# Attention followed by two feed-forward layers on one core: earlier narrowing of the first weights, a first product begun ahead of the last pair's values, and one set of subtractions moved and reordered

## The chip, the cores and the metric

The kernel runs on one core of one Trainium2 chip. The metric is device time in microseconds (us) of one execution. Before the change three runs took 783.86, 786.02 and 790.22 us, with a median of 786.02 us.

A core has five engines that run side by side, each through its own list of instructions in the order in which the program wrote them: PE (TensorE, matrix products; its weight loads are shown as PEld), DVE (VectorE), ACT (ScalarE), POOL (GpSimd) and SP (SyncE, which here issues nearly all DMAs). They wait for one another by semaphores.

## What is computed

The reference is attention with a learned bias on the position, then a feed-forward layer with a rational activation, then four ReLU experts that are mixed by given probabilities. Cut to what matters (B=2, 8 heads, S=576, head width 64; 1152 tokens of 512):

```python
scores = scale * q @ k^T + bias(pos)          # 16 pairs of (batch, head)
attn = exp(scores - max); attn /= sum(attn) + 1e-9
x = (attn @ v) as [1152, 512]
h = x @ w_in                                  # 512 -> 2048, w_in and w_out are float64
P = a0 + a1*h + a2*h^2 + a3*h^3
Q = 1 + |b0|*|h| + |b1|*h^2
x = (P / (Q + 1e-6)) @ w_out                  # 2048 -> 512
out = sum over e of p[:, e] * (relu(x @ w1[e]) @ w2[e])   # 4 experts, 512 -> 1024 -> 512
```

Products are made to float32 accuracy from operands that are split into a high part and a low part (the rest), so that each product is three passes: high by high, high by low, low by high.

## The kernel before, in words

**Attention.** The work is cut into eight pairs of heads, `pair[0]` to `pair[7]`, each of nine units `u` (score blocks of 128 rows by 576). A loop over all units in one row keeps three of them in flight: `scores` two units ahead (PE, two halves of a block into two PSUM buffers called `s`, then on DVE L527, which adds the bias and finds the minimum), `exp` one unit ahead (ACT, L536), then `weights` (DVE, a transpose, L543) and `fill` for the unit itself. `fill` puts other work into the gaps: the products with V of the pair before (`values`, PE, L576), the transposes of q and k of the pair after next (`prep`, only in pairs 0 to 5; the slot in pairs 6 and 7 is empty), the DMAs of later pairs, and POOL's `put`, which divides by the row sums and splits the result into high and low parts of `x` (L594 to L598). Work that `fill` puts on the list `later` is issued at the next unit, ahead of that unit's `exp` and transpose.

**Narrowing.** `w_in` and `w_out` arrive as 64-bit words (tile `words`) and are turned into float32 (tile `narrow`) in four steps: step 0 on ACT (L359), steps 1, 2 and 3 on DVE (L361, L363, L365); step 4 is the split (high part on ACT, L369; low part on POOL, L375). The first two weights are narrowed in four pieces during attention by `early_convert`. The list `EARLY` names the 20 units after which one step each is put on `later`. All four pieces use the one buffer `narrow0`. The loads of the two weights are issued at units (2, 4) and (3, 4), the loads of the next two at (5, 6) and (7, 3). The first piece's result goes to the buffer that held part of the bias of pairs 0 to 3.

**From attention to the first layer.** After the loop the last pair's products with V are made in two calls of `values` (blocks 0 to 4, then 5 to 17), with the first product of the feed-forward layer, `first(W1[0][0], 0)`, between them: 24 matrix products, from four slices `x_t[0]` to `x_t[3]` of the input (slice 3 comes from pairs 6 and 7), into one PSUM buffer `hp`. `chain` then makes the activation from `hp` on ACT and DVE.

**The last expert products.** Two thirds of the tokens go through the experts by a scheme of seven products in place of eight (class `Square`), on sums and differences of the blocks of `x` and of the weights. `sums_of_x` makes these sums, and splits them: high parts on ACT (L953), low parts on DVE (L956, six subtractions). It is a generator that is taken three steps further at three places. `turns(n)` makes n steps of the preparation of the next weight (for a `Group`: ACT L406 and L407, DVE L410, POOL L412 to L415, ACT L417, DVE L420). A `Square`'s first product goes to a PSUM bank `sa`, which ACT copies out (L1046) before PE writes it again.

Of the kernel before, what the change touches and what calls it, by code (L numbers as in the profile page):

```python
# [11 lines left out]
F32 = mybir.dt.float32  # L12
# [9 lines left out]
E, FE = 4, 1024  # L22
# [3 lines left out]
P = 128  # L26
# [5 lines left out]
CHN = 384  # L32
# [15 lines left out]
def attention_then_two_ffn(ctx: ExitStack, tc: tile.TileContext, q, k, v, w1, b1, w2, w_in, w_out, ca, cb, probs, e_w1, e_w2, c_l, c_l8, c_p, c_x, out):  # L48
# [6 lines left out]
    def mm(o, l, r, start, stop):  # L55
        pe.matmul(o, lhsT=l, rhs=r, start=start, stop=stop)  # L56
# [17 lines left out]
    def blk(slot, shape, dt, name):  # L74
        return long.tile(shape, dt, tag=f"blk{slot}", name=name)
# [97 lines left out]
    def catch_up(calls):  # L173
        now, calls[:] = calls[:], []
        for f in now:
            f()
# [517 lines left out]
    COPY_V.update({(n, 1): n for n in range(2, NN)})  # L694
    EARLY_LOAD = (2, 4), (3, 4)
    MORE_LOAD = (5, 6), (7, 3)
    EARLY = [divmod(t + d, 9) for t in (36, 44, 52, 60) for d in (0, 1, 2, 3, 5)]

    units = [(n, u) for n in range(NN) for u in range(9)]
    units[:11] = [(0, u) for u in (0, 1, 2, 3, 4, 5, 8)] + [(1, 0), (1, 1), (0, 6), (0, 7)]  # L700
# [19 lines left out]
            convert(5 - state["step"])  # L720
        return w.t

    def first(w, c):

        wt = ready(w)
        w.left -= 1
        hp = ps.tile([P, 2, 512], F32, tag="s", name="hp")
        for fi in range(2):
            i = 0
            for cc in range(4):  # L730
                for wpart, xpart in ((0, 0), (0, 1), (1, 0)):
                    mm(hp[:, fi, :CHN], wt[:, cc, wpart, 128 * fi:128 * fi + 128], x_t[cc][:, c, xpart], i == 0, i == 11)
                    i += 1
        return hp[:, :, :CHN]


    NGRP = len(GROUPS)
# [43 lines left out]
    last = pair[-1]  # L781
    while later:
        catch_up(later)
    last.values(range(0, 5))
    begun = chain(0, first(W1[0][0], 0), lambda name: blk(8, [P, 2, CHN], F32, name) if name == "u" else sp_.tile([P, 2, CHN], F32, tag="pq", name=name, bufs=3))
    next(begun)
    last.turn()
    last.values(range(5, NKB))
# [147 lines left out]
    def sums_of_x():  # L936


        def y(d, c):
            return yacc[:, d:d + 2, CHN * c:CHN * c + CHN]  # L940

        y11, y21, y12, y22 = y(0, T1), y(0, T2), y(2, T1), y(2, T2)
        dve.tensor_tensor(y22, y21, y22, ALU.add)
        pool.tensor_tensor(y21, y11, y21, ALU.subtract)
        dve.tensor_tensor(y11, y22, y11, ALU.subtract)
        dve.tensor_tensor(y12, y12, y11, ALU.subtract)
        yield
        sa, sb = (blk(slot, [P, 3, 2, CHN], F32R, "s") for slot in S_SLOT)
        x4 = [x_t[c][:, T2] for c in range(2)]
        split = [(y22, sa[:, 0:2]), (y11[:, 0:1], sa[:, 2:3]), (y11[:, 1:2], sb[:, 0:1]), (y21, sb[:, 1:3])] + [(y12[:, c:c + 1], x4[c].unsqueeze(1)) for c in range(2)]  # L950
        sums.extend([sa[:, 0], sa[:, 1], sa[:, 2], sb[:, 0], sb[:, 1], sb[:, 2]] + x4)
        for s, x in split:
            act.activation(x[:, :, 0], s, AF.Copy)  # L953
        yield
        for i, (s, x) in enumerate(split):
            dve.tensor_tensor(x[:, :, 1], s, f32(x[:, :, 0]), ALU.subtract)  # L956
        yield

# [5 lines left out]
    for u in range(E):  # L964
        for f2 in range(1, 4):
            if (u, f2) != (0, 1):
                expert_first(u, f2)
            turns(PACE.get(u, PACE[1])[f2 - 1])
            if 0 < u < E - 1 and results:
                results.pop(0)()  # L970
        if u + 1 < E:
            expert_first(u + 1, 0)
        for t in range(3):
            expert_second(u, t)
            if (u, t) == (E - 2, 0):
                assert not results
                making = sums_of_x()
            if (u, t) in ((E - 2, 0), (E - 1, 0), (E - 1, 1)):
                next(making)
            turns(PACE.get(u, PACE[1])[3 + t])  # L980

    ffn.close()
    psum.close()
# [159 lines left out]
```

## Time and profile before

| what | before |
|---|---|
| runs | 783.86, 786.02, 790.22 us; median 786.02 us |
| profiled execution, own time | 785.17 us |
| its span, first to last instruction | 783.4 us (1.8 us lie outside) |
| PE busy | 758.9 us, 97% of the span |
| PEld busy | 657.0 us, 84% |
| DVE busy | 550.2 us, 70% |
| ACT busy | 429.2 us, 55% |
| POOL busy | 268.0 us, 34% |
| granted TensorE clock | 0.999 of full speed (the upper level, 2.4 GHz) |
| attention with its bias | 0 to about 184 us |
| feed-forward layer | about 184 to 393 us |
| experts, first third of the tokens, then the rest | about 393 to 529 us, 529 to 783 us |

Busy time is time in which an engine works on an instruction. For PE it includes short waits inside a run of matrix products, since their ends are modelled. An engine's idle time matters only where the engine is what the others wait for; here that is mostly PE.

### The profile page before, as it was taken

How to read it: one execution, taken by the hardware profiler on the slowest of the kernel's cores; microseconds unless marked ns; L12 is line 12 of the kernel's file. 1: busy time of each engine (PE TensorE's matmuls, PEld its weight loads, DVE VectorE, ACT ScalarE, POOL GpSimd, SP SyncE). 2: the span in 40 equal slices, each digit the busy share in tenths (PEclk: the TensorE clock that was granted, in tenths of full speed). 3: DMA queues.
4: the chain of work that ended last, by engine and by line, in shares of the span. 5: the costliest groups of instructions: out<-in, count | busy, mean ns of one | idle time of the engine just before them, and what ended most of it. 6: DMA issues, size and time to landing. Idle time of an engine off the chain costs nothing. (4 is left out here: it accounts for less than half of the span.)

```text
span 783.4 us, 15914 instructions
## 1 busy us (share of the span) xinstructions
PE 758.9 (97%) x6470; PEld 657.0 (84%) x6470; DVE 550.2 (70%) x873; ACT 429.2 (55%) x689; POOL 268.0 (34%) x278
## 2 busy tenths in 40 slices
PE   7998999989999999999999999998999999999998
PEld 4445766657899999999998989988989989988987
DVE  7998878996999999999854544566545544644731
ACT  6986657765899789787823425244413423413510
POOL 0000223452354556643210101217435634723710
PEclk9999999999999999999999999999999999999999
DMA  8899587542142142402223435332212212212201
GB/s 149 193 217 213 119 191 171 133 100 65 54 124 93 57 131 83 160 3 61 74 64 126 144 101 159 108 109 95 81 48 79 85 31 82 82 42 75 73 28 54
DMA packets 83945, 79.41 MB, mean 101 GB/s; under 512 B 38016, under 2 KB 62976, under 8 KB 83200
## 3 DMA queue, kind: packets, MB, share of 16 engines
q1 hardware_dynamic: 83440, 78.39, 37.0%
q8 instruction: 51, 0.84, 0.4%
q14 instruction: 22, 0.18, 0.1%
q10 hardware_dynamic: 432, 0.01, 0.0%
HBM read 59.20 MB, written 2.36 MB: 79 GB/s over the span
## 5 line engine op out<-in xcount | busy, mean ns | idle before, releaser
L56 PE MATMUL hp<-x,wi 128*128 128x384 f32 x888 | 159.7, 337 | 1.5 <-DVE u L777 1.1
L56 PEld LDWEIGHTS hp<-x,wi 128*128 128x128 f32 x888 | 154.0, 188 | 4.1 <-PE yp L56 1.5
L56 PE MATMUL op<-w,h 128*128 128x512 f32 (+1 forms) x600 | 133.1, 382 | 0.6 <-DVE acc L895 0.6
L56 PEld LDWEIGHTS op<-w,h 128*128 128x128 f32 x600 | 109.4, 188 | 22.4 <-DVE acc L895 0.8
L56 PE MATMUL yp<-g_hi,w 128*128 128x384 f32 x384 | 102.1, 336 | 0.3 <-ACT y L832 0.3
L895 DVE SCALAR_TENSOR_TENSOR acc<-op,pr_sb,acc 128x512 f32<-128x512 f32 (+1 forms) x28 | 20.4, 730 | 72.4 <-PE op L56 72.4
L56 PEld LDWEIGHTS yp<-g_hi,w 128*128 128x128 f32 x384 | 69.7, 188 | 1.3 <-ACT yacc L824 0.7
L536 ACT ACTIVATE pq<-pq,nm 128x576 f32<-128x576 f32 x72 | 55.4, 771 | 22.2 <-DVE nm L527 21.9
L56 PE MATMUL yp<-g_lo,w 128*128 128x384 f32 x192 | 64.2, 334 | 0.0
L56 PE MATMUL sc<-ks,qs 64*128 64x288 f32 (+1 forms) x320 | 56.9, 429 | 6.4 <-DVE nm L527 4.6
L527 DVE CUSTOM_DVE_ANT_0 pq<-sc,ba 128x576 f32<-128x576 f32 x72 | 51.4, 745 | 16.2 <-PE sc L56 16.1
L417 ACT ACTIVATE wi<-stage 128x1024 fp32r<-128x1024 f32 x16 | 17.0, 1061 | 80.8 <-POOL stage L415 80.8
L373 POOL TENSOR_TENSOR w<-stage,w 128x256 fp32r<-128x256 f32 x64 | 48.2, 784 | 34.3 <-ACT w L369 34.3
L56 PE MATMUL op<-w,h_hi 128*128 128x512 f32 x192 | 59.2, 389 | 0.0
L757 POOL TENSOR_TENSOR g_lo<-u,g_hi 128x768 fp32r<-128x768 f32 x24 | 45.1, 1881 | 36.9 <-ACT g_hi L756 34.9
L369 ACT ACTIVATE w<-stage 128x1024 fp32r<-128x1024 f32 x32 | 33.6, 1054 | 37.4 <-DMA stage<-in_moe_w_dram 37.4
L543 DVE STREAM_TRANSPOSE pt<-pq 128x576 f32<-128x576 f32 x72 | 52.3, 754 | 0.0
L576 PE MATMUL o<-pt,val 32*64 32x128 f32 (+1 forms) x2304 | 48.1, 294 | 2.9 <-issue 1.7
L232 PE MATMUL bps<-hid,wb 128*32 128x288 f32 x576 | 46.9, 410 | 3.9 <-DVE hid L221 3.0
L576 PEld LDWEIGHTS o<-pt,val 32*64 32x64 f32 x2304 | 39.0, 130 | 13.0 <-issue 5.2
L56 PEld LDWEIGHTS sc<-ks,qs 64*128 64x128 f32 (+1 forms) x320 | 29.9, 175 | 23.7 <-DVE nm L527 10.1
L1036 ACT ACTIVATE h<-part_sums 128x384 fp32r<-128x384 f32 x48 | 25.1, 523 | 43.0 <-DVE part_sums L1056 34.4
(141 smaller groups left out, 1444.3 us busy)
## 6 DMA issues: line engine op xcount, KB each, us to landing
stage<-in_moe_w_dram SPq DMA_DIRECT2D x48, 512.0 KB, 3.6
ba<-ev SPq DMA_DIRECT2D x32, 288.0 KB, 5.2
words<-in_moe_w_in_dram SPq DMA_DIRECT2D x8, 1024.0 KB, 5.5
words<-in_moe_w_out_dram SPq DMA_DIRECT2D x8, 1024.0 KB, 5.0
stage<-in_moe_w_dram SPq DMA_DIRECT2D x64, 128.0 KB, 2.4
val<-val SPq DMA_DIRECT2D x21, 288.0 KB, 4.0
val<-in_v_dram SPq DMA_DIRECT2D x11, 288.0 KB, 4.5
out_dram<-acc SPq DMA_DIRECT2D x8, 256.0 KB, 2.0
```

What stands on the lines that cost most here:

```text
L56: pe.matmul(o, lhsT=l, rhs=r, start=start, stop=stop)
L232: pe.matmul(sc[32 * par:32 * par + 32, hf, :288], lhsT=wb.rearrange("p r h -> p (r h)"), rhs=tiles[par][:, 288 * hf:288 * hf + 288], start ...
L369: act.activation(t[:, :, 0, :], self.raw, AF.Copy)
L373: pool.tensor_tensor(t[:, x[0], 1, x[1]], self.raw[:, x[0], x[1]], f32(t[:, x[0], 0, x[1]]), ALU.subtract)
L417: act.activation(s[:, :, 0], raw, AF.Copy)
L527: dve.tensor_tensor_reduce(out=self.row(u + e).rearrange("p (a j) -> p a j", a=2), in0=o[:, :, :288], in1=bs.rearrange("p (a j) -> p a j", ...
L536: act.activation(self.row(u), self.row(u), AF.Exp, bias=least.pop((self.n, u)), scale=-1.0, accum_out=self.sm[:, u:u + 1])
L543: dve.transpose(self.pt[:, 5 * e + k], self.row(u))
L576: pe.matmul(self.o[64 * e:64 * e + 64, a, c:c + 32 * m], lhsT=val[self.n % 2][r, NKB * e + b], rhs=self.pt[r, i:i + m, 32 * b:32 * b + 32] ...
L757: pool.tensor_tensor(lo, u, f32(hi), ALU.subtract)
L895: dve.scalar_tensor_tensor(out=a, in0=op, scalar=pr_sb[:, j, e:e + 1], in1=a, op0=ALU.mult, op1=ALU.add)
L1036: act.activation(t[:, 0], v, AF.Relu)
```

## The change

Three places are edited. The first one moves the steps of the early narrowing: the four pieces start at global units 30, 39, 48 and 57 instead of 36, 44, 52 and 60, that is at unit 3 of pairs 3, 4, 5 and 6. The second one splits the first product of the feed-forward layer: the 18 products on slices 0 to 2 are made ahead of `values(range(0, 5))`, and the six on slice 3 stay behind it. The third one puts the last step of `sums_of_x` behind the three `turns` of its place and takes its six subtractions in another order.

```diff
-    EARLY = [divmod(t + d, 9) for t in (36, 44, 52, 60) for d in (0, 1, 2, 3, 5)]
+    EARLY = [divmod(t + d, 9) for t in (30, 39, 48, 57) for d in (0, 1, 2, 3, 5)]
...
-    def first(w, c):
+    def first(w, c, ccs=range(4), hp=None):
         wt = ready(w)
-        w.left -= 1
-        hp = ps.tile([P, 2, 512], F32, tag="s", name="hp")
+        if hp is None:
+            w.left -= 1
+            hp = ps.tile([P, 2, 512], F32, tag="s", name="hp")[:, :, :CHN]
         for fi in range(2):
-            i = 0
-            for cc in range(4):
+            for cc in ccs:
                 for wpart, xpart in ((0, 0), (0, 1), (1, 0)):
-                    mm(hp[:, fi, :CHN], wt[:, cc, wpart, 128 * fi:128 * fi + 128], x_t[cc][:, c, xpart], i == 0, i == 11)
-                    i += 1
-        return hp[:, :, :CHN]
+                    mm(hp[:, fi], wt[:, cc, wpart, 128 * fi:128 * fi + 128], x_t[cc][:, c, xpart], (cc, wpart, xpart) == (0, 0, 0), (cc, wpart) == (3, 1))
+        return hp
...
+    begun_hp = first(W1[0][0], 0, range(3))
     last.values(range(0, 5))
-    begun = chain(0, first(W1[0][0], 0), lambda name: ...
+    begun = chain(0, first(W1[0][0], 0, range(3, 4), begun_hp), lambda name: ...
...
-        for i, (s, x) in enumerate(split):
+        for s, x in split[1:4] + split[:1] + split[4:]:
             dve.tensor_tensor(x[:, :, 1], s, f32(x[:, :, 0]), ALU.subtract)
...
-            if (u, t) in ((E - 2, 0), (E - 1, 0), (E - 1, 1)):
+            if (u, t) in ((E - 2, 0), (E - 1, 0)):
                 next(making)
             turns(PACE.get(u, PACE[1])[3 + t])
+            if (u, t) == (E - 1, 1):
+                next(making)
```

On DVE, at the turn from pair 6 to pair 7, the fourth piece stood before the change as follows (`pq<-sc,ba` is L527 of one block, `pt<-pq` the transpose of one, `narrow` the piece, L548 and L549 the inverse of pair 6's sums).

```order
L361 TENSOR_SCALAR narrow<-narrow 128x512
L543 STREAM_TRANSPOSE pt<-pq 128x576
L527 ISA pq,nm<-sc,ba 128x576
L527 ISA nm 128x1
L527 ISA pq,nm<-sc,ba 128x576
L527 ISA nm 128x1
L548 TENSOR_SCALAR sm<-sm 128x9
L549 RECIPROCAL sm<-sm 128x9
L363 SCALAR_TENSOR_TENSOR narrow<-words,narrow 128x512
L543 STREAM_TRANSPOSE pt<-pq 128x576
L365 SCALAR_TENSOR_TENSOR narrow<-words,narrow 128x512
L543 STREAM_TRANSPOSE pt<-pq 128x576
```

In the changed program the fourth piece stands here, ahead of pair 6's inverse.

```order
L361 TENSOR_SCALAR narrow<-narrow 128x512
L543 STREAM_TRANSPOSE pt<-pq 128x576
L527 ISA pq,nm<-sc,ba 128x576
L527 ISA nm 128x1
L363 SCALAR_TENSOR_TENSOR narrow<-words,narrow 128x512
L543 STREAM_TRANSPOSE pt<-pq 128x576
L527 ISA pq,nm<-sc,ba 128x576
L527 ISA nm 128x1
L527 ISA pq,nm<-sc,ba 128x576
L527 ISA nm 128x1
L365 SCALAR_TENSOR_TENSOR narrow<-words,narrow 128x512
L543 STREAM_TRANSPOSE pt<-pq 128x576 x2
```

The first step stood between the transposes of units 7 and 8 of pair 6 and now stands between those of units 4 and 5; the second and third stood behind the inverse, among the first units of pair 7, and now stand ahead of the transposes of units 6 and 7. The other three pieces stand in the same way in pairs 3, 4 and 5.

On DVE, where the first third of the tokens ends in the experts, the six subtractions L956 stood before the change between two accumulations L895 and ahead of the Group's L410.

```order
L895 SCALAR_TENSOR_TENSOR acc<-op,pr_sb,acc 128x512
L956 TENSOR_TENSOR s<-yacc,s 128x2x384
L956 TENSOR_TENSOR s<-yacc,s 128x384 x2
L956 TENSOR_TENSOR s<-yacc,s 128x2x384
L956 TENSOR_TENSOR x_1345<-yacc,x_1345 128x384
L956 TENSOR_TENSOR x_1872<-yacc,x_1872 128x384
L410 TENSOR_TENSOR wi<-stage,wi 128x256 x3
L895 SCALAR_TENSOR_TENSOR acc<-op,pr_sb,acc 128x512
L420 TENSOR_TENSOR wi<-stage,wi 128x4x256
```

In the changed program the same place reads:

```order
L895 SCALAR_TENSOR_TENSOR acc<-op,pr_sb,acc 128x512
L410 TENSOR_TENSOR wi<-stage,wi 128x256 x3
L956 TENSOR_TENSOR s<-yacc,s 128x384 x2
L956 TENSOR_TENSOR s<-yacc,s 128x2x384 x2
L956 TENSOR_TENSOR x_1345<-yacc,x_1345 128x384
L956 TENSOR_TENSOR x_1877<-yacc,x_1877 128x384
L895 SCALAR_TENSOR_TENSOR acc<-op,pr_sb,acc 128x512
L420 TENSOR_TENSOR wi<-stage,wi 128x4x256
```

The three L410 went ahead of the six L956, and of the six the two short ones on `s` come first, in the order in which the products take them. ACT and POOL hold the same instructions there in the same order as before.

## Rows read from the trace of the kernel before

**Rows 1.** Busy time by stretch: from:to, length, then each engine's busy time (instructions).

```profile
149.30:164.40 15.10, 13.75 (x334) 9.32 (x334) 13.97 (x33) 11.11 (x28) 6.57 (x9) 1.00 0.46 106
164.40:180.40 16.00, 13.24 (x342) 9.25 (x350) 15.33 (x34) 9.95 (x25) 6.95 (x9) 1.00 0.54 135
```

**Rows 2.** Timeline, PE, pairs 6 and 7: start, length, work, [idle before, ended by].

```profile
159.15 1.91 PE L56 MATMUL sc<-ks,qs 64*128 64x288 f32 x8 [0.73 <-DVE nm L527]
165.12 1.24 PE L56 MATMUL sc<-ks,qs 64*128 64x288 f32 x8 [0.74 <-DVE nm L527]
169.62 1.62 PE L576 MATMUL o<-pt,val 32*64 32x160 f32 x80 [0.50 <-issue]
175.53 1.91 PE L56 MATMUL sc<-ks,qs 64*128 64x288 f32 x8 [1.54 <-DVE nm L527]
```

**Rows 3.** Busy time by stretch of what touches `narrow`: DVE, ACT, POOL.

```profile
149.30:164.40 15.10, 2.07 (x3) 1.32 (x2) 1.28 (x1) 1.00 0.46 106
164.40:180.40 16.00, 2.79 (x3) 1.30 (x2) 1.26 (x1) 1.00 0.54 135
```

**Rows 4.** Timeline, DVE, three narrowing steps.

```profile
144.79 0.64 DVE L365 SCALAR_TENSOR_TENSOR narrow<-words,narrow 128x512 uint32<-128x512 uint32 x1
...
168.45 0.38 DVE L361 TENSOR_SCALAR narrow<-narrow 128x512 uint32<-128x512 uint32 x1
...
172.75 1.37 DVE L365 SCALAR_TENSOR_TENSOR narrow<-words,narrow 128x512 uint32<-128x512 uint32 x1
```

**Rows 5.** Timeline, POOL, when the last of these steps began.

```profile
172.57 1.00 POOL L598 TENSOR_TENSOR x<-x,x 128x384 fp32r<-128x384 f32 x1
```

**Rows 6.** Timeline, DVE, unit 8 of pair 3.

```profile
117.56 0.76 DVE L527 CUSTOM_DVE_ANT_0 pq<-sc,ba 128x576 f32<-128x576 f32 x1 [0.94 <-PE sc L56]
```

**Rows 7.** Timeline, SP, the first weight's load.

```profile
99.80 0.58 SPq L340 DMA_DIRECT2D words<-in_moe_w_in_dram  x1
```

**Rows 8.** One tile's instructions (`words`), 95 to 180 us: its loads.

```profile
DMA to landing us min/median/max: 5.5/6.8/8.3
```

**Rows 9.** Timeline, ACT, an `exp` of pair 3's unit 5.

```profile
112.48 0.76 ACT L536 ACTIVATE pq<-pq,nm 128x576 f32<-128x576 f32 x1
```

**Rows 10.** Timeline, PE, from attention to the first layer.

```profile
180.27 1.64 PE L576 MATMUL o<-pt,val 32*64 32x160 f32 x80
183.03 1.64 PE L576 MATMUL o<-pt,val 32*64 32x160 f32 x80 [1.12 <-ACT x L589]
184.60 4.46 PE L56 MATMUL hp<-x,w 128*128 128x384 f32 x24
...
199.88 4.43 PE L56 MATMUL hp<-x,w 128*128 128x384 f32 x24 [0.85 <-DVE u L777]
```

**Rows 11.** Timeline, POOL, low part of slice 3 of `x`.

```profile
185.18 1.06 POOL L598 TENSOR_TENSOR x<-x,x 128x384 fp32r<-128x384 f32 x1
```

**Rows 12.** Timeline, DVE, around the six subtractions.

```profile
517.83 1.66 DVE L410 TENSOR_TENSOR wi<-stage,wi 128x256 fp32r<-128x256 f32 x3
...
524.65 2.75 DVE L956 TENSOR_TENSOR s<-yacc,s 128x768 fp32r<-128x768 f32 x4
...
528.26 1.09 DVE L410 TENSOR_TENSOR wi<-stage,wi 128x256 fp32r<-128x256 f32 x3
...
533.51 1.23 DVE L420 TENSOR_TENSOR wi<-stage,wi 128x1024 fp32r<-128x1024 f32 x1 [3.49 <-ACT wi L417]
```

**Rows 13.** Timeline, POOL, the Group's four subtractions: first and last.

```profile
528.76 1.19 POOL L412 TENSOR_TENSOR stage<-stage 128x256 f32<-128x256 f32 x1 [7.04 <-DVE wi L410]
...
531.66 0.72 POOL L415 TENSOR_TENSOR stage<-stage 128x256 f32<-128x256 f32 x1
```

**Rows 14.** Timeline, ACT, behind them.

```profile
532.42 1.06 ACT L417 ACTIVATE wi<-stage 128x1024 fp32r<-128x1024 f32 x1 [8.77 <-POOL stage L415]
```

**Rows 15.** Timeline, PE, the same stretch.

```profile
533.90 1.32 PE L1024 MATMUL sa<-x,wi 128*128 128x384 f32 x6 [1.96 <-ACT part_sums L1046]
535.25 1.31 PE L1024 MATMUL sb<-s,wi 128*128 128x384 f32 x6
```

More of the change, by code (lines that the diff above doesn't have):

```diff
@@ L783, in attention_then_two_ffn @@
         catch_up(later)
+    begun_hp = first(W1[0][0], 0, range(3))
     last.values(range(0, 5))
-    begun = chain(0, first(W1[0][0], 0), lambda name: blk(8, [P, 2, CHN], F32, name) if name == "u" else sp_.tile([P, 2, CHN], F32, tag="pq", name=name, bufs=3))
+    begun = chain(0, first(W1[0][0], 0, range(3, 4), begun_hp), lambda name: blk(8, [P, 2, CHN], F32, name) if name == "u" else sp_.tile([P, 2, CHN], F32, tag="pq", name=name, bufs=3))
     next(begun)
```

## The prediction

> **What bounds the kernel now.** I read the share of busy time first: PE works 97% of the span, so a change can gain little more than PE's waits. The list of who waited for whom came next, for PE alone, and PE's timeline to place its waits. Behind the first 80 us most of them lie in three places: in attention's second half, at its end, and at one point in the experts. The chain of waits that ended last is PE alone from 533.9 us to the end, so a shift ahead of that point carries through to the end as long as nothing else becomes late. The granted clock is at the upper level throughout.
>
> Pairs 6 and 7 are the first place. In the two stretches from 149.3 to 180.4 us, 31.1 us long, DVE is busy 29.3 us and PE 27.0 us [rows 1]: DVE is the bound. On PE the reader is to see four waits, 0.73 + 0.74 + 0.50 + 1.54 = 3.51 us [rows 2]. Three end with a `nm` of L527, that is with DVE; I count the one put down to "issue" with them, since these values need pair 6's last transpose, which DVE makes right behind the L361 of 168.45 [rows 4]. In pairs 0 to 5 PE also makes `prep`, so that there DVE waits for PE: 0.94 us ahead of unit 8 of pair 3 [rows 6].
>
> The second place is the end of attention: PE stands idle 1.12 us until ACT has emptied the value bank, then makes values, then the 24 products of `hp` in 4.46 us [rows 10]. The third is a wait of 1.96 us for ACT's L1046 [rows 15]. ACT was held by L417, that by POOL's L412 to L415, those by DVE's L410, and L410 stood behind the six L956 [rows 12, 13, 14].
>
> **First edit, the steps of the narrowing.** No step is added or removed; 12 steps on DVE, 4 on ACT and 4 splits move. In the 31.1 us two pieces stand on DVE, busy 2.07 + 2.79 = 4.86 us [rows 3]. Afterwards only one stands there, the fourth, since the third moves into pair 5. Its price where POOL is idle: 0.38 us for L361, 0.64 us for L365, and the same 0.64 us for L363, which has the same form [rows 4]: 1.66 us. The old price held waits: L365 at 172.75 took 1.37 us, and until 173.57 POOL's L598 was at work [rows 4, 5]. The new places, units 4 to 6, lie ahead of POOL's `put`, which starts after unit 7. So DVE loses 4.86 - 1.66 = 3.20 us, less about 0.07 us by which each of the three steps that leave overlapped its successor: 3.0 us. DVE would then need 26.3 us and PE 27.0 us, which includes short waits; neither is far ahead of the other. I take the gain as DVE's relief, **3.0 us**. From below it is 1.5 us, if only the wait at 175.53 goes; from above 3.5 us, if all four waits of rows 2 go.
>
> What the moved steps cost in pairs 3, 4 and 5: the first piece is new in pair 3, and each piece stands at units 4 to 6. Its second and third step (0.64 us each) precede transposes that nobody on PE needs at once, and DVE's idle time ahead of unit 8 is 0.94 us [rows 6]. I take nothing; without that cover it is 1.66 us a pair. On ACT step 0 (0.65 us, half of ACT's share in rows 3) goes ahead of the `exp` at 112.48 [rows 9]; ACT is idle 4 us of the 15.1 us of a stretch with a piece [rows 1]. It reads the first weight, issued at 99.80 [rows 7], landed at the latest 8.3 us after its issue [rows 8], so by 108.1: 4.4 us early. The single buffer `narrow0` is free again long before the next piece, since POOL's split (1.27 us [rows 3]) follows at the start of the next pair, ahead of nothing but the next `put`, most of a pair later. The load at (7, 3), until now held on SP by the fourth piece's L365, may leave sooner; no other DMA queues behind it before the first layer.
>
> **Second edit, the first product.** The 18 products need no new data: slices 0 to 2 come from pairs 0 to 5, and the PSUM buffer is the one that L527 of unit 8 left. They cost 4.46 / 24 = 0.186 us each, 3.3 us together, and take the place of the wait of 1.12 us; the rest of them is only moved ahead of the values. So the gain is **1.1 us**. It is lost if the six products on slice 3 must wait: they start 3.3 + 1.6 = 4.9 us after the previous values end at 181.9, at 186.8, and the low part of slice 3 was ready at 185.18 + 1.06 = 186.24 [rows 11]. The margin is 0.6 us; the value lies between 0 and 1.1 us. Nothing later takes it back: the activation's chain, `put_last` and the product at 199.88 that waits for L777 [rows 10] all hang on these products and values and move with them.
>
> **Third edit, the subtractions.** PE's wait would go if L412 to L415 ended two us earlier. L410 moves ahead of L956 by the length of the six, 528.26 - 524.65 = 3.6 us [rows 12]. But L412 reads and writes SBUF, and so do L410 and L956, and rows 12 and 13 show that these exclude each other. L412 was started at 528.76, when one L410 was done, and took 1.19 us instead of 0.72: it ended at 529.95, as if it had begun at 529.2, when the third L410 had ended. It waited out two DVE instructions, which follow each other without a gap. After the change the same three L410 are followed without a gap by six L956. If POOL waits out all nine, L412 starts at 524.65 + 1.0 + 3.6 = 529.3, as before, and the edit gives nothing. That is my value: **0 us**. The other bound is the whole wait, 1.96 us, and 0.3 us that the next product (535.25, six products of 0.174 us after 533.90) lost to L1048: 2.3 us.
>
> The Trainium skill, page "SBUF — State Buffer", section "Who interferes with whom", says that a VectorE instruction with two SBUF inputs and a GpSimd instruction that reads SBUF exclude each other, and that whoever issues first holds the pair of ports for one whole instruction. By it L412 would have come in after the second L410; the trace shows it after the third. By the page POOL and DVE would take turns here, which is the first rival below.
>
> **Sum.** The profiled execution took 785.17 us, 1.8 us of it outside the span; 785.17 - 3.0 - 1.1 - 0 = **781.1 us**. It is 0.85 us under the median of the runs shown.
>
> **Rivals.**
>
> *POOL and DVE take turns.* For it: at 517.83 the same three L410 took 1.66 us instead of 1.09 [rows 12], because an L412 came in ahead of the third. Against it: the wait at 528.76. Worked out: L412 to L415 at 0.74 us, an L410 or a short L956 (about 0.4 us) between each two, from 525.1 on, end at about 528.9; L417 ends at 530.0; L1046 is done ahead of 531.8, where PE needs it. DVE then ends L956 at 531.5, makes an L895 (0.7), L420 (1.2 [rows 12]) and L1048 (0.5), so that the product of 535.25 starts at 533.85: 1.4 us gained, **779.7 us**.
>
> *Pairs 6 and 7 find another limit.* PE and DVE feed each other in turns through two PSUM buffers, so that only the wait at 175.53 goes: 785.17 - 1.5 - 1.1 = **782.6 us**.
>
> *Slice 3 comes late.* The second edit gives nothing: 785.17 - 3.0 = **782.2 us**.
>
> *Slower: the narrowing holds up pairs 3 to 5.* Step 2 now stands right behind L527 of unit 8, and step 3 right behind that of the next pair's units 0 and 1; if the transposes behind them are what the next values on PE wait for, each of the three pairs pays the piece's whole 1.66 us, 5.0 us together, and the kernel takes 785.17 - 4.1 + 5.0 = **786.1 us**. It decides from 1.4 us a pair on. For it: DVE is busy most of the time there too. Against it: the idle time in rows 6, just where the steps go.
>
> **How the numbers follow.** I give the forecast 0.45, turns of POOL and DVE 0.25, another limit 0.13, slice 3 late 0.08, the slower case 0.09. The predicted time is 781.1 us. From 778.9 (all of 3.5, 1.1 and a part of the third edit) to 783.7 (1.5 us alone), widened by the 0.85 us between the profiled execution and the median, the range is 778.0 to 784.6 us; it leaves out the slower case and little more. About 1% (7.9 us) is what a measurement of this kernel tells from no change. All upper bounds together, 3.5 + 1.1 + 2.3 = 6.9 us, stay under that, so faster by over 1% gets 0.08, within 1% 0.88 and slower 0.04.
>
> **What would show it.** In the changed profile the stretch between the `rt` products (L561) of pairs 5 and 7 should be about 3 us shorter, and the waits of rows 2 be under 1 us together, with L363 and L365 at about 0.65 us each. Ahead of the values at the end of attention 18 `hp` products should stand without a wait of PE. L412 should start some 3.6 us earlier and still end behind the last L956, with L1046 and PE's wait of 2 us unchanged. The prediction is wrong if the gain of pairs 6 and 7 turns up again as waits in pairs 3 to 5, or if PE's wait for L1046 is gone.

## The result and the profile after

The changed kernel takes 781.05 us (median of 8 runs, 778.51 to 782.72), the kernel before 786.25 us beside it (8 runs). The ratio is 0.992, with a 95% interval of 0.989 to 0.995: 5.2 us less, within 1%. The forecast of 781.1 us lies on the median, but not every term under it was right, and things that I did not forecast took part.

The profiled execution took 778.81 us (span 777.0 us), 6.36 us less than that of before. PE's busy time is what it was, 758.7 us, so all of it is PE's waits. The page's head of the changed kernel (busy us, share of the span, instructions):

```profile
PE 758.7 (98%) x6470; PEld 657.5 (85%) x6470; DVE 551.3 (71%) x873; ACT 428.9 (55%) x689; POOL 266.8 (34%) x278
```

To find where the 6.4 us went I cut both executions at the same PE instructions: the first `rt` product (L561) made in each pair, and the first, seventh and thirteenth product into `sa` of the `Square`s. Ahead of the first cut (100.97 us in both) nothing differs, and behind the last one both need 246.98 us.

| stretch (us) | before | after | difference |
|---|---|---|---|
| `rt` in pair 2 to `rt` in pair 5 | 47.45 | 45.79 | -1.66 |
| `rt` in pair 5 to `rt` in pair 7 | 31.09 | 28.48 | -2.61 |
| `rt` in pair 7 to the last turn's | 9.38 | 8.90 | -0.48 |
| from there to the first `sa` product | 339.75 | 339.61 | -0.14 |
| first to thirteenth `sa` product | 7.75 | 6.25 | -1.50 |

**Pairs 5 to 7.** The two stretches by busy time (from:to, length, then PE, PEld, DVE, ACT, POOL with their instructions, granted clock, share of DMA, GB/s), cut at the `rt` products, of before and then of after; they answer to [rows 1]:

```profile
148.42:163.55 15.13, 13.75 (x336) 9.32 (x334) 14.00 (x32) 10.65 (x28) 6.57 (x9) 1.00 0.52 129
163.55:179.51 15.96, 13.18 (x336) 9.12 (x335) 15.29 (x34) 10.10 (x25) 6.95 (x9) 1.00 0.49 113
```

```profile
146.76:160.26 13.50, 13.11 (x337) 9.12 (x335) 13.15 (x31) 9.54 (x25) 6.03 (x9) 1.00 0.56 140
160.26:175.24 14.98, 13.26 (x336) 9.23 (x335) 14.21 (x33) 10.26 (x26) 6.04 (x9) 1.00 0.45 94
```

DVE is busy 1.93 us less and idle 0.68 us less; together that is the 2.61 us. It is still busy 27.4 of 28.5 us. PE's waits in the changed kernel, from its timeline (start, length, work, [idle before, ended by]), which answer to [rows 2]:

```profile
162.03 1.65 PE L56 MATMUL sc<-ks,qs 64*128 64x288 f32 x8 [0.95 <-DVE nm L527]
...
166.80 1.62 PE L576 MATMUL o<-pt,val 32*64 32x160 f32 x80 [0.38 <-issue]
...
170.70 1.30 PE L576 MATMUL o<-pt,val 32*64 32x160 f32 x50 [0.40 <-issue]
```

Four waits of 3.51 us became three of 1.73 us, and the long one ahead of the last scores is gone. The forecast had wanted them under 1 us together. The twelve steps on DVE, seen as one tile's instructions (`narrow`; ns: shortest, median, longest), answer to [rows 3, 4]:

```profile
L361 DVE TENSOR_SCALAR narrow<-narrow x4: 383/384/386, 114.8 to 160.2; 128x512 uint32<-128x512 uint32 x4
L363 DVE SCALAR_TENSOR_TENSOR narrow<-words,narrow x4: 685/687/689, 117.1 to 161.9; 128x512 uint32<-128x512 uint32 x4
L365 DVE SCALAR_TENSOR_TENSOR narrow<-words,narrow x4: 686/686/686, 120.1 to 164.7; 128x512 uint32<-128x512 uint32 x4
```

No step takes longer than 0.69 us any more, where L365 took 1.37 us beside POOL.

**The end of attention.** PE's timeline, which answers to [rows 10]:

```profile
176.00 2.15 PE L576 MATMUL o<-pt,val 32*64 32x160 f32 x80
178.07 3.39 PE L56 MATMUL hp<-x,w 128*128 128x384 f32 x18
181.40 1.64 PE L576 MATMUL o<-pt,val 32*64 32x160 f32 x80
182.97 1.34 PE L56 MATMUL hp<-x,w 128*128 128x384 f32 x6
```

The 18 products stand where the wait of 1.12 us was, and nothing waits from 176 to 184 us. But the 80 value products at 176.00 take 2.15 us, half a microsecond more than in [rows 10]. The first edit alone will show where that belongs.

**The experts.** DVE, then POOL, then ACT, then PE in the changed kernel, which answer to [rows 12 to 15]. L1046 and L1048 of before are L1048 and L1050 here:

```profile
519.61 1.62 DVE L410 TENSOR_TENSOR wi<-stage,wi 128x256 fp32r<-128x256 f32 x3
521.15 4.39 DVE L956 TENSOR_TENSOR s<-yacc,s 128x384 fp32r<-128x384 f32 x4
525.47 1.01 DVE L956 TENSOR_TENSOR x<-yacc,x 128x384 fp32r<-128x384 f32 x2
526.40 0.74 DVE L895 SCALAR_TENSOR_TENSOR acc<-op,pr_sb,acc 128x512 f32<-128x512 f32 x1
527.07 1.27 DVE L420 TENSOR_TENSOR wi<-stage,wi 128x1024 fp32r<-128x1024 f32 x1
528.26 0.54 DVE L1050 TENSOR_TENSOR part_sums<-sb,part_sums 128x384 f32<-128x384 f32 x1
```

```profile
520.10 0.84 POOL L412 TENSOR_TENSOR stage<-stage 128x256 f32<-128x256 f32 x1 [3.72 <-DVE wi L410]
...
522.92 0.94 POOL L415 TENSOR_TENSOR stage<-stage 128x256 f32<-128x256 f32 x1
```

```profile
525.00 0.49 ACT L1048 ACTIVATE part_sums<-sa 128x384 f32<-128x384 f32 x1
```

```profile
526.88 1.20 PE L1026 MATMUL sa<-x,wi 128*128 128x384 f32 x6
528.86 1.31 PE L1026 MATMUL sb<-s,wi 128*128 128x384 f32 x6 [0.78 <-DVE part_sums L1050]
```

POOL's L412 to L415 are done at 523.86, in the midst of the L956. ACT empties `sa` by 525.5, PE writes it at 526.88 without a wait, and what is late next is `sb`: 0.78 us for L1050, which stands on DVE behind all six L956, L895 and L420. The four L956 on `s` take 4.39 us beside POOL, against 2.75 us alone [rows 12].

### The profile page after: what moved, and what is told of

It is laid out like the page before. It is cut to its first block, busy times and chain, and to the rows that moved or that the text cites. A ratio compares the mean times of both kernels' runs of the same rounds, so it can differ in the third digit from the quotient of the medians.

```text
span 777.0 us, 15918 instructions
## 1 busy us (share of the span) xinstructions
PE 758.7 (98%) x6470; PEld 657.5 (85%) x6470; DVE 551.3 (71%) x873; ACT 428.9 (55%) x689; POOL 266.8 (34%) x278
## 5 line engine op out<-in xcount | busy, mean ns | idle before, releaser
L895 DVE SCALAR_TENSOR_TENSOR acc<-op,pr_sb,acc 128x512 f32<-128x512 f32 (+1 forms) x28 | 20.4, 730 | 72.8 <-PE op L56 72.8
L527 DVE CUSTOM_DVE_ANT_0 pq<-sc,ba 128x576 f32<-128x576 f32 x72 | 51.6, 749 | 13.3 <-PE sc L56 13.1
L417 ACT ACTIVATE wi<-stage 128x1024 fp32r<-128x1024 f32 x16 | 17.0, 1061 | 77.8 <-POOL stage L415 77.8
L576 PE MATMUL o<-pt,val 32*64 32x160 f32 (+1 forms) x2304 | 48.8, 293 | 2.3 <-issue 1.9
L221 DVE TENSOR_SCALAR hid<-tab,cut 128x576 f32<-128x576 f32 x112 | 48.4, 522 | 0.0
```

The costliest lines, as they stand in the source:

```text
L221: dve.tensor_scalar(tiles[par], win, at, 0.0, ALU.add, ALU.max)
L527: dve.tensor_tensor_reduce(out=self.row(u + e).rearrange("p (a j) -> p a j", a=2), in0=o[:, :, :288], in1=bs.rearrange("p (a j) -> p a j", ...
L576: pe.matmul(self.o[64 * e:64 * e + 64, a, c:c + 32 * m], lhsT=val[self.n % 2][r, NKB * e + b], rhs=self.pt[r, i:i + m, 32 * b:32 * b + 32] ...
```

## The experiments

### Each edit alone

The first edit alone:

```diff
-    EARLY = [divmod(t + d, 9) for t in (36, 44, 52, 60) for d in (0, 1, 2, 3, 5)]
+    EARLY = [divmod(t + d, 9) for t in (30, 39, 48, 57) for d in (0, 1, 2, 3, 5)]
```

> The kernel before with the first edit alone (the 20 narrowing steps at the new units). The forecast's own step: pairs 6 and 7 lose 3.0 us, pairs 3 to 5 nothing, so ratio 0.996. Rival: the wait of PE of 1.15 us in pair 3, which the changed kernel's profile no longer has, went because of the moved steps; then 4.3 us and ratio 0.9945. If it was chance, that wait may stand in this trace too. The wait of 1.12 us ahead of the last pair's values and that of 1.96 us for L1046 should both stand as before.

Measured: 783.92 us, ratio 0.9961 (0.9940 to 0.9982). The `rt` products in pairs 5 and 7 are 28.46 us apart, 2.63 us less than before. Pairs 2 to 5 need 47.46 us, as before. But the stretch from pair 7's `rt` to the last turn's grew from 9.38 to 9.91 us, so 2.1 us are left of the 2.63 us. PE's timeline has the slower values of the changed kernel here too, although nothing is split:

```profile
177.64 2.15 PE L576 MATMUL o<-pt,val 32*64 32x160 f32 x80
```

The second edit alone:

```diff
+    begun_hp = first(W1[0][0], 0, range(3))
     last.values(range(0, 5))
-    begun = chain(0, first(W1[0][0], 0), lambda name: ...
+    begun = chain(0, first(W1[0][0], 0, range(3, 4), begun_hp), lambda name: ...
```

> The kernel before with the second edit alone (18 products ahead of the last pair's values). Forecast: the wait of 1.12 us for ACT's L589 goes and nothing takes it back, ratio 0.9986. From the rt products of pair 7 to the last rt products it should take 9.38 - 1.1 = 8.3 us. Rival: the 0.5 us that only came off in the changed kernel's profile (9.38 to 8.90) is all there is, since the values ahead of it lose 0.5 us each time; then 8.9 us here too.

Measured: 786.07 us, ratio 0.9986 (0.9967 to 1.0005). From pair 7's `rt` to the last turn's 8.37 us, 1.01 us less. So it gives its whole price by itself, which the medians alone would not have told.

The third edit alone:

```diff
-        for i, (s, x) in enumerate(split):
+        for s, x in split[1:4] + split[:1] + split[4:]:
...
-            if (u, t) in ((E - 2, 0), (E - 1, 0), (E - 1, 1)):
+            if (u, t) in ((E - 2, 0), (E - 1, 0)):
                 next(making)
             turns(PACE.get(u, PACE[1])[3 + t])
+            if (u, t) == (E - 1, 1):
+                next(making)
```

> The kernel before with the third edit alone (subtractions moved behind the Group's steps and reordered). Forecast: POOL waits out all nine DVE instructions, L412 ends as late as before and PE's wait of 1.96 us stays: 0 us, ratio 1.000. Rival, which the changed kernel's profile speaks for: POOL and DVE take turns, the wait of 1.96 us goes and one of about 0.8 us for the sum on sb (L1048) comes: 1.5 us, ratio 0.998.

Measured: 784.44 us, ratio 0.9964 (0.9943 to 0.9986). First to thirteenth `sa` product 6.26 us, 1.49 us less, with one wait of 0.79 us for L1050. The edit that I had put at nothing gives the second most of the three.

### Which half of the third edit

The move alone, in the old order:

```diff
-            if (u, t) in ((E - 2, 0), (E - 1, 0), (E - 1, 1)):
+            if (u, t) in ((E - 2, 0), (E - 1, 0)):
                 next(making)
             turns(PACE.get(u, PACE[1])[3 + t])
+            if (u, t) == (E - 1, 1):
+                next(making)
```

> The kernel before with one half of the third edit: the step with the six subtractions stands behind the three turns, but the subtractions keep their old order, with the long one (128x2x384, 1.1 us) first and the two short ones that the first products take second and third. Theory one, what counts is that L410 and with it L412 to L415, L417 and L1046 come ahead: PE's wait of 1.96 us for L1046 [rows 15] becomes less than 0.3 us, and from the first to the thirteenth sa product 6.2 to 6.5 us are needed instead of 7.75 (1.3 to 1.5 us gained), as with the whole edit, unless a product waits for its low part. Theory two, the order matters: PE gains a wait for DVE's L956 of 0.5 us or more in the first Square's second half, and the stretch takes 6.7 to 7.3 us. Rival that I took in the prediction (POOL waits out all nine DVE instructions): 7.7 us; the whole edit alone has shown 6.26 us, so that it should not return here.

The new order alone, in the old place:

```diff
-        for i, (s, x) in enumerate(split):
+        for s, x in split[1:4] + split[:1] + split[4:]:
```

> The kernel before with the other half of the third edit: the six subtractions in the new order, but still ahead of the three turns. Theory one, L410 still stands behind six L956 on DVE, so L412 to L415 start as late as before and PE's wait for L1046 stays: 1.96 us, give or take 0.3, and 7.6 to 7.8 us from the first to the thirteenth sa product. Theory two, the gain came from the products finding their low parts earlier: the stretch gets at least 0.5 us shorter. It also shows whether POOL's first L412 waits out two L410 each time at this place (1.19 us in rows 13) or comes in ahead of the third L410, as it did at 517.83 [rows 12].

Measured: the move takes 784.66 us, ratio 0.9978 (0.9960 to 0.9996), the order 786.85 us, ratio 1.0008 (0.9987 to 1.0028). With the move the stretch of the `sa` products is 6.51 us, and PE waits once, 1.03 us for L1050. Its timeline, DVE and PE:

```profile
528.56 1.62 DVE L410 TENSOR_TENSOR wi<-stage,wi 128x256 fp32r<-128x256 f32 x3
...
530.11 4.39 DVE L956 TENSOR_TENSOR s<-yacc,s 128x768 fp32r<-128x768 f32 x4
```

```profile
538.06 1.32 PE L1026 MATMUL sb<-s,wi 128*128 128x384 f32 x6 [1.03 <-DVE part_sums L1050]
```

No product waits for a low part, so theory one holds: the move gives 1.24 of the 1.50 us and the order at most the rest. With the order alone, DVE, POOL and PE:

```profile
526.51 1.09 DVE L410 TENSOR_TENSOR wi<-stage,wi 128x256 fp32r<-128x256 f32 x3
...
527.01 1.20 POOL L412 TENSOR_TENSOR stage<-stage 128x256 f32<-128x256 f32 x1 [7.03 <-DVE wi L410]
...
532.17 1.32 PE L1024 MATMUL sa<-x,wi 128*128 128x384 f32 x6 [1.88 <-ACT part_sums L1046]
```

The wait for L1046 is there nearly whole, 1.88 us. The stretch takes 8.60 us, not the expected 7.6 to 7.8 us, since the clock fell to the lower level behind this wait, at 533.43 us, for 3.4 us. L412 again takes 1.20 us while the three L410 take 1.09 us: in the old place POOL waits out two L410, not by chance. Everywhere else it does not. In the kernel before there are ten more places at which an L412 starts while three L410 stand in a row, and at all ten it came in ahead of the third. One of them, DVE and POOL:

```profile
570.81 1.63 DVE L410 TENSOR_TENSOR wi<-stage,wi 128x256 fp32r<-128x256 f32 x3
```

```profile
571.36 0.80 POOL L412 TENSOR_TENSOR stage<-stage 128x256 f32<-128x256 f32 x1 [9.61 <-issue]
```

What sets the old place apart is open: L412 starts 0.5 us behind the first L410 at both kinds of place.

### The last two subtractions later still

The changed kernel with its last two L956 (low parts of two blocks of `x`) issued inside the first `Square`, behind the sum that L1050 makes:

```diff
-        for s, x in split[1:4] + split[:1] + split[4:]:
+        for s, x in split[1:4] + split[:1]:
+            dve.tensor_tensor(x[:, :, 1], s, f32(x[:, :, 0]), ALU.subtract)
+        yield
+        for s, x in split[4:]:
             dve.tensor_tensor(x[:, :, 1], s, f32(x[:, :, 0]), ALU.subtract)
...
+                if (self.e, self.g, m) == (0, 0, 2):
+                    next(making)
```

> The changed kernel with the last two of the six subtractions (those on x, 0.47 us each) taken out of their place and issued behind the first sum of the Square's second product, where nothing waits for them. Theory: what is left of PE's wait (0.78 us) is DVE being late by these two, the accumulation L895 and L420; without the two it shrinks by up to 0.78 us: 0.999 of the changed kernel, about 0.991 of the kernel before. Rival: DVE then waits for ACT's L417 and POOL instead, and the 0.78 us stay.

Measured: 780.38 us (6 runs), ratio 0.9905 (0.9877 to 0.9933). No wait is left; the stretch is 5.26 us, 1.0 us less than with the change. So the 0.78 us at 528.86 was the price of the last two L956, as the theory had it, and the rival (a wait for L417 and POOL in their place) is out. It is the fastest kernel of the study; its median is 0.67 us under that of the changed one, less than the medians tell apart, and the trace carries the claim.

### Which pieces of the narrowing pay

The fourth piece alone moved ahead of POOL's `put`; the third stays in the stretch:

```diff
-    EARLY = [divmod(t + d, 9) for t in (36, 44, 52, 60) for d in (0, 1, 2, 3, 5)]
+    EARLY = [divmod(t + d, 9) for t in (36, 44, 50, 57) for d in (0, 1, 2, 3, 5)]
```

> The kernel before with only the fourth piece of the narrowing moved ahead of POOL's put (it starts at unit 3 of pair 6); the first two pieces stay, and the third starts two units earlier than before, so that it and the fourth both stay in the stretches of pairs 6 and 7 (149 to 180 us), where DVE is the bound. Theory one, the relief goes by DVE's time: the fourth piece falls from 2.79 us [rows 3] to about 1.7 us, the third still costs its 2.1 us, so the time from the rt products of pair 5 to those of pair 7, 31.09 us before and 28.48 us with the whole change, becomes 30.0 us (1.0 to 1.3 us gained). Theory two, the wait at 175.53 [rows 2] alone was worth something and the third piece was hidden: 28.5 to 29.5 us. Theory three, only the piece that leaves the stretch counts: 31 us. Whole time by theory one 785.2, against 786.3 for the kernel before.

The first three moved, the fourth left:

```diff
-    EARLY = [divmod(t + d, 9) for t in (36, 44, 52, 60) for d in (0, 1, 2, 3, 5)]
+    EARLY = [divmod(t + d, 9) for t in (30, 39, 48, 60) for d in (0, 1, 2, 3, 5)]
```

> The kernel before with the first three pieces moved as in the change and the fourth left where it was (behind pair 6's last units, beside POOL's put). Theory one, the relief goes by DVE's time: the third piece's 2.07 us [rows 3] leave the 31.09 us between the rt products of pairs 5 and 7, the fourth keeps its 2.79 us, so they become 29.2 to 29.6 us. Theory two, the wait at 175.53 [rows 2], which the fourth piece makes, stays and was all that counted: 30.5 to 31 us. With theory one this run and the one with the fourth alone should add up to the 2.6 us of the first edit. Pairs 3 to 5 pay nothing (47.4 us from the rt products of pair 2 to those of pair 5, give or take the waits put to issue, which are 0 to 1.8 us). Whole time by theory one 784.5, against 786.3.

Measured: the fourth alone takes 785.55 us, ratio 0.9980 (0.9961 to 0.9999), the first three 785.02 us, ratio 0.9990 (0.9970 to 1.0009). With the fourth alone the `rt` products are 15.24 + 14.46 = 29.70 us apart, 1.39 us less, a little more than theory one gave (1.0 to 1.3 us). But DVE's relief alone does not make it. In the part that holds the fourth piece DVE is busy 0.90 us less and 1.50 us are gained; in the other part the third piece's L365 now stands beside POOL's L598 and takes 1.43 us, DVE is busy 0.57 us more, and 0.11 us are lost. The difference is idle time of DVE. With the first three moved the `rt` products are 13.49 + 17.55 = 31.04 us apart. That looks like this run's theory two, but isn't. The first part has gained 1.64 us; in the second the granted clock fell. Windows (columns as above) and PE's timeline:

```profile
174.00:176.00 2.00, 1.31 (x6) 0.83 (x7) 2.00 (x6) 1.27 (x3) 1.49 (x2) 0.92 1.07 221
176.00:178.00 2.00, 2.00 (x28) 1.10 (x34) 1.88 (x5) 0.94 (x3) 0.00 (x0) 0.50 0.67 175
178.00:180.27 2.27, 2.27 (x48) 1.21 (x33) 1.56 (x4) 1.11 (x4) 0.00 (x0) 0.76 0.84 319
```

```profile
174.69 2.71 PE L56 MATMUL sc<-ks,qs 64*128 64x288 f32 x8 [1.67 <-DVE nm L527]
177.34 1.89 PE L576 MATMUL o<-pt,val 32*64 32x160 f32 x48
```

Behind the wait of 1.67 us PE ran at 0.50, the lower level (1.2 GHz), for about 3.4 us; the 48 products took 1.89 us instead of 1.09 us. The kernel with the subtractions only moved has the narrowing of before and such a fall at the same place, and needs 17.58 us for this part instead of 15.96: the fall costs 1.6 us. Without it the first three pieces would give about 31.04 - 1.6 = 29.4 us, as theory one has it; that is worked out, not measured. Both pieces pay, by 1.4 and about 1.6 us; their sum of 3.0 us is somewhat over the 2.6 us of the whole edit.

### What the two other edits take from each other, and the clock

The changed kernel with the first edit undone:

```diff
-    EARLY = [divmod(t + d, 9) for t in (30, 39, 48, 57) for d in (0, 1, 2, 3, 5)]
+    EARLY = [divmod(t + d, 9) for t in (36, 44, 52, 60) for d in (0, 1, 2, 3, 5)]
```

> The changed kernel with the first edit undone: the narrowing stands where it stood before, the first product is split and the subtractions are moved. Theory one, on the first product: its gain of 1.0 us shows whole only where the steps are not moved, since the moved steps bring a stall of 0.5 us in the values ahead of the 18 products (PE at 176.00 in the changed kernel, 2.15 us instead of 1.64 us for the same 80 products). Then the time between the rt products of pair 7 and those of the last pair is 8.3 to 8.4 us here, against 8.90 us in the changed kernel; the rival, that the 18 products themselves bring the stall, gives 8.9 us. Theory two, on TensorE's clock: its falls to the lower level (1.2 GHz, about 3.3 us long) come in some executions behind waits of 1.5 us and more on PE, of which the kernel before has one in pair 7 and one at L1046. With the one in pair 7 alone the mean granted clock of the twelve runs should lie between the 0.9966 of the kernel before and the 0.9990 of the changed one, at about 0.998; if the falls have nothing to do with these waits, it stays at 0.999 or at 0.997. Time: 783.0 to 784.0 us by theory two, 782.5 us without more falls.

The changed kernel with the third edit undone:

```diff
-        for s, x in split[1:4] + split[:1] + split[4:]:
+        for s, x in split:
...
-            if (u, t) in ((E - 2, 0), (E - 1, 0)):
+            if (u, t) in ((E - 2, 0), (E - 1, 0), (E - 1, 1)):
                 next(making)
             turns(PACE.get(u, PACE[1])[3 + t])
-            if (u, t) == (E - 1, 1):
-                next(making)
```

> The changed kernel with the third edit undone: the six subtractions stand ahead of the three turns again, in the old order. The wait for L1046 returns at 1.8 to 2.0 us and the time from the first to the thirteenth sa product is 7.6 to 7.8 us in an execution at the full clock, 1.4 to 1.5 us more than in the changed kernel. On TensorE's clock: by the theory that its falls come in some executions behind waits of 1.5 us and more, the mean granted clock of the twelve runs is about 0.998 (one such place, at L1046, in place of two in the kernel before and none in the changed one), and the median is 0.5 to 1.0 us above what the trace shows, at 783.0 to 783.6 us; by the rival, that they come anywhere, the mean clock stays at 0.999 and the median is 782.5 us.

Measured: without the steps 783.87 us, ratio 0.9967 (0.9946 to 0.9988); without the subtractions 782.45 us, ratio 0.9950 (0.9930 to 0.9970). Without the steps, PE at the end of attention:

```profile
182.03 1.64 PE L576 MATMUL o<-pt,val 32*64 32x160 f32 x80
183.60 3.40 PE L56 MATMUL hp<-x,w 128*128 128x384 f32 x18
```

The values take 1.64 us and the stretch 8.37 us, as theory one said. But the split gives its 1.01 us either way: from 9.38 to 8.37 us without the moved steps, from 9.91 us (first edit alone) to 8.90 us with them. So the two edits take nothing from each other; the first one gives back 0.5 us of its own gain, behind the `rt` product of pair 7. In the five profiled kernels with all pieces or the last one moved, this stretch is 0.5 to 0.6 us longer than with the same first product and the last piece in its old place, or 1.1 us in the one with the later subtractions.

No semaphore releases the stall, but the traces' DMA packets show what came just ahead of it. The page of the changed kernel counts them (packets, MB, share of the 16 DMA engines):

```profile
q8 instruction: 51, 0.84, 0.4%
```

These 51 packets of 16,384 bytes face 13,046 recorded instructions of PE and PEld, about 256 for each packet. In the changed kernel the 23rd of them landed at 175.16, and the stalled product started 1.4 us later, at 176.55. In the four kernels that stall at this product it is 1.2 to 1.6 us; in the other eight, where the product does not stall, the packet had landed 2.0 to 6.5 us ahead. With the fourth piece alone the stall (0.45 us) comes 256 instructions later, 1.5 us behind the next packet. So PE waited for its own instructions, by everything that these traces show; no run changed their arrival, and why the packet comes so close here is open.

Without the subtractions PE waits 1.83 us for L1046 again. The stretch is 8.87 us there, not the 7.6 to 7.8 us of an execution at the full clock: the clock fell behind the wait.

On the clock: the kernel before has two places with a long wait, in pair 7 (1.54 us, in some executions less) and at L1046 (1.96 us). The mean granted clock over all runs of a kernel follows how many of the two its program still has:

| places left | kernels | mean granted clock |
|---|---|---|
| both | before (83 runs), second edit alone, order alone, first three pieces | 0.9964 to 0.9966 |
| one | first edit alone, third edit alone, move alone, fourth piece alone, without the steps, without the subtractions | 0.9972 to 0.9982 |
| none | the changed kernel, the one with later subtractions | 0.9985 to 0.9990 |

By the scatter of the runs the standard error of these means (how far off such a mean may well be) is 0.0002 for the first row (119 runs), 0.0003 for the second (68) and 0.0005 for the third (14). So the step from 0.9965 to 0.9979 is clear, and that from 0.9979 to 0.9988 is not. The two new kernels lie between the rows above and below (0.9972 and 0.9978), but with 12 and 8 runs and a standard error of 0.0009 neither decides by itself. The median without the subtractions, 782.45 us, is what the rival expected. And the two places are not all: three of the eight falls in the profiled executions came behind a wait in pair 3 that every kernel can have (last section). So theory two is supported by the sum of the kernels, not shown by these two.

## Why the prediction was right, and where it was not

**First edit, 3.0 us forecast, 2.6 us measured between the `rt` products, 2.1 us with what follows.** The mechanism held: DVE was the bound, POOL's `put` was what made the steps long, and the waits at `nm` fell from 3.0 to 0.95 us. The first step that failed is "Afterwards only one stands there". Between the `rt` products DVE still spends 3.13 us on `narrow` (five steps), not 1.66 us: two steps of the third piece, at 147.56 and 150.49, still lie behind the `rt` product at 146.76. DVE's relief on the narrowing was 1.73 us and on all its work 1.93 us; the other 0.68 us of the 2.6 us came from shorter waits of DVE. So 3.0 us came near 2.6 us by two errors that partly cancel: DVE's relief was put too high, and the waits' part of the gain was left out. The second step that failed is a term left out: what the moved steps cost was sought in pairs 3 to 5 alone, and behind pair 7's `rt` product PE lost 0.5 us with them. Net, the first edit gave 2.1 us. My unit prices (0.64 us for L363 and L365) were 0.05 us low.

**Pairs 3 to 5, nothing forecast, nothing measured.** PE's waits there, before (90 to 149 us) and after (90 to 146.8 us), by line (engine, line, what was waited for: us, times, longest):

```profile
PE sc L56 <- issue: 1.1, 1, 1.1
PE o L576 <- issue: 0.5, 1, 0.5
```

```profile
PE o L576 <- ACT x L589: 0.3, 1, 0.3
PE o L576 <- issue: 0.3, 1, 0.3
```

The slower rival is out: no wait for DVE or for a transpose appears. The 1.66 us that these pairs gained in the profiled execution is not the change's. It is two waits put to "issue" that this one execution did not have. The first edit alone, with the same list on all engines there, still has them (0.83 and 0.87 us), and the new order alone, with the narrowing of before, lacks them.

**Second edit, 1.1 us forecast, 1.0 us measured, alone and beside the first.** Slice 3 was not late: its L598, which answers to [rows 11], ended at 182.45, and the six products at 182.97 did not wait. The forecast margin was 0.6 us, the measured one 0.5 us:

```profile
181.45 1.00 POOL L598 TENSOR_TENSOR x<-x,x 128x384 fp32r<-128x384 f32 x1
```

"Nothing later takes it back" held: the stall that hides half of it in the table comes earlier, in the values ahead of the 18 products, and belongs to the moved steps, since the first edit alone has it.

**Third edit, nothing forecast, 1.5 us measured.** The failed step is "If POOL waits out all nine". By the prediction's own sign ("if PE's wait for L1046 is gone") this term was wrong. It made a rule out of one row [rows 13], while the same trace held ten places that spoke against it, and I weighed one of those only as a rival. The row was also read too sharply: the third L410 ended at 528.26 + 1.09 = 529.35, not at 529.2. In its new place L412 came in ahead of the third L410, as the rival "POOL and DVE take turns" said. Put on the time of before (4.90 us later, by the first `sa` product), the rival's steps were L415's end at 528.9 (measured 528.76), L956's end at 531.5 (531.38) and the `sb` product at 533.85 (533.76). The Trainium skill, page "SBUF — State Buffer", section "Who interferes with whom", says that whoever issues first holds the shared ports for its whole instruction; the trace of the changed kernel agrees, with L412 to L415 of 0.84, 0.80, 0.94 and 0.94 us among the L410 and L956. At the old place L412 waited out two instructions, with 1.19 and 1.20 us, and what decided there is open.

**The sum.** By edits the trace gives 2.1 + 1.0 + 1.5 = 4.6 us against the 4.1 us forecast, so the errors nearly cancelled. The medians differ by 5.2 us. The rest is in the start of the sum: I subtracted from the profiled execution of before (785.17 us), 1.1 us under the median beside the result, and its clock was at the upper level throughout. Of 83 runs of the kernel before, 13 had a mean granted clock of 1.000, with a median of 784.18 us; all together have 786.66 us. Five of the changed kernel's eight runs had 1.000, with 780.57 us (778.51 to 782.22). Too few runs stand behind that difference of 3.6 us, but all 201 runs whose clock is on record can be used: within one kernel, 0.001 less of the mean clock goes with 0.60 us more. With that taken off, the changed kernel is 4.6 us faster than the one before (standard error 0.5 us), the first edit alone 1.9 us (0.3), the second 0.7 us (0.3) and the third 1.3 us (0.3), which agrees with the trace. The clock adds its part to this: the means differ by 0.0025, which is 1.5 us by the same slope, an estimate. The two together, 6.1 us, lie inside the interval of the measured ratio (4.2 to 8.5 us). The clock's gain is not in the lengths of the waits, and neither the forecast nor a rival named it. That the forecast met the median is partly luck: a gain 1.1 us too small was taken from a start 1.1 us too low.

## What to carry to other kernels

Before a contention is priced from a row, look up every place of the trace where the same two instructions meet; the exception here stood just where the edit was made. Count which steps of a moved piece really leave the stretch whose bound is relieved, by the cut at which the gain will be read. A long wait of PE can cost more than its length, so the sum should start from runs at the same granted clock. Where PE stands idle and no semaphore releases it, look at the packets of the instruction queue. And before one edit's gain is said to be eaten by another, measure each with and without the other.

## What was not expected of the hardware

**Falls of the clock behind waits.** In the twelve profiled executions eight falls to the lower level occurred behind the first 80 us, each about 3.4 us long. Each began 0.2 to 2.1 us after PE had resumed from a wait, of 1.22 to 1.88 us. But of the 19 waits of PE that were at least 1.2 us long, 11 were not followed by one, the two of before among them (1.54 and 1.96 us). So a single profile may or may not show a fall, and what decides is not shown. With the second edit alone, PE and the windows around it:

```profile
533.62 2.15 PE L1024 MATMUL sa<-x,wi 128*128 128x384 f32 x6 [1.83 <-ACT part_sums L1046]
535.57 1.96 PE L1024 MATMUL sb<-s,wi 128*128 128x384 f32 x6
```

```profile
532.00:534.00 2.00, 0.38 (x2) 0.38 (x3) 0.78 (x1) 1.86 (x3) 0.10 (x1) 0.95 0.00 0
534.00:536.00 2.00, 2.00 (x8) 2.00 (x7) 0.92 (x2) 0.65 (x2) 1.41 (x3) 0.50 0.24 31
```

Six products take 1.96 us where they take 1.20 us at the upper level, and the seventh to the thirteenth `sa` product 3.76 us instead of 2.50 us.

**A wait at one place that comes and goes.** At one product of the scores in pair 3, PE stands idle in most executions, and no semaphore releases it. Before and second edit alone:

```profile
110.05 0.99 PE L56 MATMUL sc<-ks,qs 64*128 64x288 f32 x5 [1.15 <-issue]
```

```profile
110.84 0.99 PE L56 MATMUL sc<-ks,qs 64*128 64x288 f32 x5 [1.77 <-issue]
```

In the profiled executions of the changed kernel and of the new order alone it is missing. It is worth up to 1.8 us of one execution and has nothing to do with the edit under study. It is another wait for instructions. This product and five other places with waits of this kind (in pair 4 at about 127 us, in pair 7, twice among the values at the end of attention, and some 5 us behind the last `rt` product) stand at multiples of 256 instructions, give or take one, from one another in PE's list. In each of the twelve traces these waits end 1.2 to 1.9 us after a packet of the instruction queue has landed. In the ten with the wait in pair 3 the packet landed at 108.1 to 109.6; in the other two it landed at 107.4 and 106.8, 1.5 and 1.7 us ahead of the product, and no idle time is shown. That the packet's time decides is read from this order in time; what makes the packet early or late was not tried.
